# Strips' maxima combined by one reduction, softmax sums in two levels, and a new order table, in a fused attention and mixture-of-experts kernel

## The chip, the core and the metric

The kernel runs on one core of one Trainium2 chip. The metric is the device time of one execution in microseconds. TensorE is called PE below, VectorE DVE, ScalarE ACT, GpSimd POOL and SyncE SP, as in the profile. PSUM is the memory that PE writes, in eight banks; SBUF is the main on-chip memory.

## What is computed

Two attentions with 32 inducing points, and then a mixture of experts on the result. B = 4 batches of N = 11456 tokens, C = 128 channels, m = 32, E = 8 experts, F = 1024.

```python
def _attn_ref(x, inducing):
    def mab(q, kv):
        s = scale * (q @ kv.transpose(0, 2, 1))
        s = s - s.max(-1, keepdims=True)
        a = np.exp(s)
        a /= a.sum(-1, keepdims=True) + 1e-09
        return a @ kv
    h = mab(I, x)          # first attention: 32 queries over all tokens
    return mab(x, h)       # second attention: every token over 32 keys

def _moe_ref(x, w_skip, w_gate, w1, w2):   # x: the attention's output, all tokens
    do_compute = x @ w_skip > 0
    # a token that computes takes its best expert e of x @ w_gate:
    # out = x + prob_e * relu(x @ w1[e]) @ w2[e]; the others: out = x
```

## The kernel before

**Tiling.** A batch is cut into six groups of 2048 tokens (the last has 1216). The tokens of a group are laid out as four strips of 32 rows each, so that the 32 inducing points of every strip fill the 128 partitions. Most steps take two groups at once (1024 columns in each partition).

**First attention** (`first`), 13 steps in all: four in batch 0, whose first two groups go singly, and three in each other batch. A step is: scores on PE (L397, L400), the largest score of each partition on DVE (`maxima`, L404, stored negated in a column of the small tile `mins`), the combination of the four strips' values and of the older minimum into one value for each of the 32 rows and its spread back to all 128 partitions (`least`, L409 to L418, six short DVE instructions: copies of 64 and 32 rows to other partitions and element-wise minima), the exponentials on ACT with that value as bias (L421, and L424 for the factor that rescales older sums), a transpose of 32x32 blocks on DVE (L431), transposes of x on PE (L439) copied out by ACT or DVE (`copy`, L344 and L346), sums on PE (L453), and their addition to `acc` on DVE (L462).

**Middle** (`middle`), once for each batch: h from `acc` (PE L502, DVE L506, L507), the expert that the batch mostly takes, its weights by two DMAs on SP's queue (`load_w`, L665, L667), and the expert's image of the 32 rows of h.

**Second attention** (`second`), 13 steps: scores (L692), transpose to tokens on DVE (L696), greatest of each token's 32 (L700), its subtraction (`less`, L708, in two halves, one for each group, on POOL or DVE), exponentials on ACT into the tile `texp` (L711), the sums of 32 values and a constant 1e-9 as a 33rd column on DVE (`total`, L715), the reciprocal (L717), the scaling (`norm`, L721, two halves on POOL or DVE), a transpose (L726), the gate logits and gate (L734 to L776), a second scaling (`scale2`, L782, two halves) and transpose (L726), and `emit`: the output's sums on PE (L822), the copies out of PSUM, and the stores on SP's queue.

**Order.** Nothing is scheduled by the compiler. `ORDER` holds, for each engine, the numbers of the steps in the order in which that engine's instructions stand; which engine runs a step with a choice (`less`, `norm`, `scale2`, copies out of PSUM) follows from the list in which its number stands. `placed` replays these lists with the costs that each step is given, and so chooses the PSUM banks and buffers. The costs (`both`, `dve`, `act` and the dictionaries at `L.add`) choose nothing else: the engines run their lists in order on the chip and wait for each other by semaphores. `awake` puts idle matmuls ahead of a PE step where that replay shows a gap on PE.

Of the kernel before, what the change touches and what calls it, by code (L numbers as in the profile page):

```python
# [1168 lines left out]
```

## Time and profile before

| | before |
|---|---|
| median of 3 runs | 200.16 us (199.42 to 200.36) |
| the profiled execution | 199.29 us, span 197.3 us |
| busy, of the span | PE 178.8 us (91%), DVE 166.3 (84%), ACT 119.5 (61%), POOL 102.1 (52%) |
| granted TensorE clock | 0.99 of full speed, mean |
| DMA | 51.54 MB, mean 261 GB/s |

The span runs from the first to the last instruction of the profiled execution; 2.0 us of its time lie outside the span. The page gives busy times, the chain that ended last, and groups of instructions by line; the trace behind it gives each stretch of time, each line and each wait. Matmuls overlap, so PE's busy time holds some time in which PE drains.

### The profile page before, as it was taken

The page shows a single profiled execution, that of the slowest core. Times are in us where ns is not written, and L with a number is a line of the kernel's source. Part 1 is how long each engine was busy: PE and PEld are TensorE (multiplying, and loading weights), DVE is VectorE, ACT ScalarE, POOL GpSimd, SP SyncE. Part 2 cuts the span into 40 slices and gives each one's busy share as a digit, 9 for nine tenths or more (in the row PEclk, how much of TensorE's full clock was granted, in tenths as well). Part 3 has the DMA queues.
Part 4 walks back from the last instruction along what each step waited for, and adds up shares of the span by engine and source line. Part 5 has one row for each costly group of instructions (what it writes and reads, how often), then busy time and mean ns, then how long its engine had stood idle before and what let it go on. Part 6 is the DMA issues. An engine that isn't in the chain of part 4 may idle for free. (4 is left out here: it accounts for less than half of the span.)

```text
span 197.3 us, 5919 instructions
## 1 busy us (share of the span) xinstructions
PE 178.8 (91%) x2353; PEld 111.3 (56%) x2354; DVE 166.3 (84%) x367; ACT 119.5 (61%) x179; POOL 102.1 (52%) x194
## 2 busy tenths in 40 slices
PE   7997999997999899999889998999999959999972
PEld 7565667445874755756466356677435334453641
DVE  0699788899999999999999979998988983998641
ACT  3215324334876583884759539765959557789780
POOL 8000000274449561988456177656987895567430
PEclk9999999999999999999999999999999996999999
DMA  6999990199900003999903949375189998798996
GB/s 211 374 420 403 410 379 23 40 397 388 404 16 5 3 0 118 327 399 394 389 21 112 381 154 325 130 196 223 71 350 357 279 401 343 308 355 324 406 375 233
DMA packets 16317, 51.54 MB, mean 261 GB/s; under 512 B 1952, under 2 KB 4000, under 8 KB 16288
## 3 DMA queue, kind: packets, MB, share of 16 engines
q1 hardware_dynamic: 16000, 51.12, 69.1%
q8 instruction: 19, 0.31, 0.6%
q14 instruction: 10, 0.08, 0.1%
q10 hardware_dynamic: 288, 0.02, 0.1%
HBM read 27.68 MB, written 23.46 MB: 259 GB/s over the span
## 5 line engine op out<-in xcount | busy, mean ns | idle before, releaser
L344 ACT COPY o<-bank 128x1024 f32<-128x1024 f32 (+1 forms) x48 | 44.3, 961 | 15.6 <-PE bank L822 8.7
L439 PE MATMUL bank<-ident,x 128*128 128x128 f32 x360 | 47.3, 279 | 2.2 <-DVE e L696 1.4
L344 ACT COPY xt<-bank 128x1024 f32<-128x1024 f32 (+3 forms) x44 | 37.3, 889 | 13.0 <-PE bank L439 7.0
L439 PEld LDWEIGHTS bank<-ident,x 128*128 128x128 f32 x360 | 39.4, 141 | 9.9 <-issue 2.8
L822 PE MATMUL bank<-x,hr 32*128 32x512 f32 (+1 forms) x192 | 27.8, 615 | 3.6 <-ACT o L344 2.8
L708 POOL TENSOR_TENSOR e<-e,ts 128x512 f32<-128x512 f32 (+1 forms) x24 | 23.9, 1011 | 13.4 <-DVE ts L700 12.0
L721 POOL TENSOR_TENSOR e<-texp,ts 128x512 f32<-128x512 f32 (+1 forms) x24 | 23.9, 1012 | 11.3 <-DVE ts L717 10.2
L726 DVE STREAM_TRANSPOSE x<-e 128x1024 f32<-128x1024 f32 (+3 forms) x26 | 28.4, 1098 | 1.5 <-POOL e L782 0.9
L421 ACT ACTIVATE a<-bank,mins 128x1024 f32<-128x1024 f32 (+3 forms) x13 | 13.0, 1003 | 23.7 <-DVE mins L418 23.7
L453 PE MATMUL bank<-xt,a1T 128*32 128x129 f32 x720 | 24.9, 274 | 1.6 <-DVE a1T L431 1.4
L822 PE MATMUL bank<-x,yr 32*128 32x512 f32 (+1 forms) x192 | 26.2, 580 | 0.1
L453 PEld LDWEIGHTS bank<-xt,a1T 128*32 128x32 f32 x720 | 20.0, 110 | 9.7 <-issue 5.6
L782 POOL TENSOR_TENSOR e<-e,gs 128x512 f32<-128x512 f32 (+1 forms) x20 | 20.4, 1032 | 7.1 <-DVE gs L346 4.0
L397 PE MATMUL bank<-x,iT_sb 128*32 128x512 f32 (+1 forms) x192 | 22.0, 567 | 1.5 <-DMA x<-in_xT_dram 0.7
L692 PE MATMUL bank<-x,hc 128*32 128x512 f32 (+1 forms) x192 | 22.3, 578 | 0.1
L587 POOL TENSOR_SCALAR r<-codes,code,lr 128x7 f32<-128x7 f32 x4 | 1.7, 425 | 33.0 <-DVE lr L577 33.0
L696 DVE STREAM_TRANSPOSE e<-bank 128x1024 f32<-128x1024 f32 (+3 forms) x13 | 14.4, 1111 | 4.7 <-ACT o L344 3.0
L822 PEld LDWEIGHTS bank<-x,hr 32*128 32x128 f32 x192 | 9.7, 188 | 13.3 <-ACT o L344 4.6
L711 ACT ACTIVATE texp<-e 128x1024 f32<-128x1024 f32 (+3 forms) x13 | 12.6, 968 | 7.0 <-DVE e L696 4.3
L822 PEld LDWEIGHTS bank<-x,yr 32*128 32x128 f32 x192 | 11.0, 191 | 9.7 <-issue 8.5
L431 DVE STREAM_TRANSPOSE a1T<-a 128x1024 f32<-128x1024 f32 (+3 forms) x13 | 14.2, 1094 | 1.4 <-ACT a L421 1.3
L404 DVE TENSOR_REDUCE mins<-bank 128x1 f32<-128x1024 f32 (+3 forms) x13 | 13.7, 1057 | 1.4 <-PE bank L397 1.2
(132 smaller groups left out, 229.8 us busy)
## 6 DMA issues: line engine op xcount, KB each, us to landing
x<-in_xT_dram SPq DMA_DIRECT2D x40, 512.0 KB, 9.1
out_dram<-o SPq DMA_DIRECT2D x40, 512.0 KB, 3.6
out_dram<-o SPq DMA_DIRECT2D x8, 304.0 KB, 5.0
w1s<-in_w_dram SPq DMA_DIRECT2D x4, 512.0 KB, 5.0
w2s<-in_w_dram SPq DMA_DIRECT2D x4, 512.0 KB, 5.2
x<-in_xT_dram SPq DMA_DIRECT2D x4, 320.0 KB, 5.1
x<-in_xT_dram SPq DMA_DIRECT2D x4, 288.0 KB, 4.4
iT_sb<-in_iT_dram ACTq DMA_DIRECT2D x1, 16.0 KB, 3.0
```

Of the source, the lines that this page charges most:

```text
L344: nc.scalar.copy(out=out, in_=in_)
L397: nc.tensor.matmul(ps[q * M:(q + 1) * M, off[i]:off[i] + G.kf * M], lhsT=iT_sb, rhs=x[:, q], start=True, stop=True)
L431: nc.vector.transpose(out=st["aT"][:, 0:W], in_=st["a"][:, 0:W])
L439: nc.tensor.transpose(out=at(buf)[0:w, j * P:(j + 1) * P], in_=s.x[gs[i]][:, k * P:k * P + w], identity=ident)
L453: nc.tensor.matmul(ph[k % Q * M:(k % Q + 1) * M, 0:P + 1], lhsT=st["aT"][:, c:c + M], rhs=flat(i)[:, k, :], start=(i == 0 and k < Q), stop ...
L692: nc.tensor.matmul(ps[q * M:(q + 1) * M, off[i]:off[i] + G.w2], lhsT=s.hc[:, 0:M], rhs=s.x[g][:, G.s2[q]:G.s2[q] + G.w2], start=True, stop ...
L696: nc.vector.transpose(out=st["e"], in_=st["ps"][:, 0:W])
L708: on(o).tensor_tensor(out=v, in0=v, in1=part(st["mx"], i), op=ALU.subtract)
L721: on(o).tensor_tensor(out=blocks(st["e"], i), in0=texps[bex.idx][:, t0:t0 + Gs[i].nb, 0:M], in1=part(st["i"], i), op=ALU.mult)
L726: nc.vector.transpose(out=u[:, 0:W], in_=st["e"])
L782: on(o).tensor_tensor(out=v, in0=v, in1=gm.unsqueeze(3).broadcast_to([P, Q, v1 - v0, M]), op=ALU.mult)
L822: nc.tensor.matmul(at(bp[q // 2])[:, p0:p0 + G.w1], lhsT=m[r, :], rhs=st[k][r, c], start=(k == "u1"), stop=(k == "u2"))
```

## The change

**The combination of maxima.** `mins` gets Q + 2 = 6 columns and is made one step ahead. `maxima` still writes column 0. A new step `gather` copies the values of strips 1 to 3 into columns 1 to 3 of the first 32 partitions (three copies of 32x1, on POOL or ACT). `least` is one DVE reduction over these columns and, except in a batch's first step, over column 4, where the step before left its minimum. A new step `spread` copies the result to the other three strips, and, except after a batch's last step, into column 4 of the next step's tile (three or four copies of 32x1, on POOL or ACT).

**The sums of the second attention.** `texp` holds each token's 32 exponentials as two halves of 16, with a 17th column each (1e-9 and 0). A new POOL step `fold` adds the two halves, 17 columns for each token, into `e`, and `total` reduces 17 columns instead of 33.

**Weights.** The two weight DMAs become two steps of SP's list; the first product waits for the first alone in the planner.

**Order and costs.** `ORDER` is new in every engine's list, and some costs are changed.

```diff
     "DVE": """
-9 14 4 5 16 7 21 26 28 13 22 45 24 38 39 30 48 41 60 61 63 65 72 70 52 203 74 204 76 77 79 80 206 82 85 97 98 128
+4 11 6 16 30 9 23 25 32 15 28 51 42 44 54 18 47 34 66 68 71 58 78 215 82 217 84 85 87 220 106 107 88 108 239 138 139
...
-    texps = [const.tile([P, PB, M + 1], F32, name=f"texp{i}") for i in range(BUFS["ex"])]
+    texps = [const.tile([P, PB, 2, M // 2 + 1], F32, name=f"texp{i}") for i in range(BUFS["ex"])]
     for t in texps:
-        nc.gpsimd.memset(t[:, :, M:M + 1], 1e-9)
+        nc.gpsimd.memset(t[:, :, 0, M // 2:], 1e-9)
+        nc.gpsimd.memset(t[:, :, 1, M // 2:], 0.0)
...
+        def gather(o):
+            for q in range(1, Q):
+                copy(o, mins[0:M, q:q + 1], mins[q * M:(q + 1) * M, 0:1])
+
         def least(o):
-
-            m, v = mins[:, 0:1], mins[:, 2:4]
-            nc.vector.tensor_copy(out=v[0:2 * M, 0:1], in_=m[2 * M:4 * M])
-            nc.vector.tensor_tensor(out=v[0:2 * M, 1:2], in0=m[0:2 * M], in1=v[0:2 * M, 0:1], op=ALU.min)
-            nc.vector.tensor_copy(out=v[0:M, 0:1], in_=v[M:2 * M, 1:2])
-            if one:
-                nc.vector.tensor_tensor(out=bias[0:M], in0=v[0:M, 0:1], in1=v[0:M, 1:2], op=ALU.min)
-            else:
-                nc.vector.tensor_scalar(out=bias[0:M], in0=v[0:M, 0:1], scalar1=v[0:M, 1:2], scalar2=old[0:M],
-                                        op0=ALU.min, op1=ALU.min)
-            nc.vector.tensor_copy(out=bias[M:2 * M], in_=bias[0:M])
-            nc.vector.tensor_copy(out=bias[2 * M:4 * M], in_=bias[0:2 * M])
+            nc.vector.tensor_reduce(out=bias[0:M], in_=mins[0:M, 0:Q if one else Q + 1], axis=AX.X, op=ALU.min)
+
+        def spread(o):
+            for q in range(1, Q):
+                copy(o, bias[q * M:(q + 1) * M], bias[0:M])
+            if gs[-1] < NG - 1:
+                copy(o, after[0:M, Q:Q + 1], bias[0:M])
...
-        s.lastm = o = L.add({"DVE": 0.86}, least, o, s.lastm)
+        o = L.add({"POOL": 0.45, "ACT": 0.6}, gather, o)
+        s.lastm = o = L.add({"DVE": 0.2}, least, o, s.lastm)
+        s.lastm = o = L.add({"POOL": 0.5, "ACT": 0.75}, spread, o)
...
-        o_w = L.add({"SP": 1.6}, weights, o, take=[bw], size=1048.0)
+        o_w = [L.add({"SP": c}, lambda o, k=k: weights(o, k), o, take=[bw] if k == 1 else [], size=524.0)
+               for k, c in ((1, 0.6), (2, 0.95))]
...
         def exps(o):
-            nc.scalar.activation(out=ev(M), in_=blocks(st["e"]), func=AF.Exp, scale=scale)
+            nc.scalar.activation(out=ev(), in_=halved(blocks(st["e"])), func=AF.Exp, scale=scale)
+
+        def fold(o):
+            v = texps[bex.idx][:, 0:nb]
+            st["half"] = st["e"][:, 0:nb * (M // 2 + 1)].rearrange("p (t m) -> p t m", m=M // 2 + 1)
+            nc.gpsimd.tensor_tensor(out=st["half"], in0=v[:, :, 0, :], in1=v[:, :, 1, :], op=ALU.add)
 
         def total(o):
             r = sums[:, b, base]
-            nc.vector.tensor_reduce(out=r, in_=ev(M + 1), axis=AX.X, op=ALU.add)
+            nc.vector.tensor_reduce(out=r, in_=st["half"], axis=AX.X, op=ALU.add)
```

**Where instructions move.** The rows below are instructions as they stand in the built program: line, operation, output and inputs with the program's names, partitions x elements, and in brackets the engines that are waited for. Line numbers of after are its own. `mins_0_180` and `mins_0_166` are the `mins` tiles of batch 1's first step; `e`, `ts`, `texp` and `sums` are tiles of the second attention.

DVE at the end of batch 0's first attention, where `acc` is completed and the middle begins; before:

```order
L404 TENSOR_REDUCE mins_0_180<-bank_67 128x1 [waits PE_49]
L462 SCALAR_TENSOR_TENSOR acc_287<-acc_287,f_0_4_420,bank_69 128x129 [waits DVE_49,PE_49]
L409 COPY mins_0_180<-mins_0_180 64x1 [waits DVE_49]
L410 TENSOR_TENSOR mins_0_180<-mins_0_180 64x1 [waits DVE_49]
L411 COPY mins_0_180<-mins_0_180 32x1 [waits DVE_49]
L413 TENSOR_TENSOR mins_0_180<-mins_0_180 32x1 [waits DVE_49]
L417 COPY mins_0_180<-mins_0_180 32x1 [waits DVE_49]
L418 COPY mins_0_180<-mins_0_180 64x1 [waits DVE_49]
L506 TENSOR_SCALAR den_525<-bank_69 128x1 [waits PE_49]
```

The same place after:

```order
L409 TENSOR_REDUCE mins_0_166<-bank_68 128x1 [waits PE_49]
L466 SCALAR_TENSOR_TENSOR acc_297<-acc_297,f_0_4_435,bank_70 128x129 [waits DVE_49,PE_49,Activation_49]
L416 TENSOR_REDUCE mins_0_166<-mins_0_166 32x1 [waits DVE_49,Activation_49]
L512 TENSOR_SCALAR den_537<-bank_70 128x1 [waits PE_49]
L513 RECIPROCAL den_537<-den_537 128x1 [waits DVE_49]
```

Six DVE instructions between the last addition to `acc` and the denominator have become one, which waits for ACT's three copies.

POOL in batch 2's first step, between the gate scalings of batch 0 (L797), after; DVE's list has L409 and L416 of `mins_0_170` one behind the other there:

```order
L797 TENSOR_TENSOR e_0_1_561<-e_0_1_561,gs_0_139 128x384 [waits Activation_49]
L352 COPY mins_0_170<-mins_0_170 32x1 [waits DVE_49,Pool_49]
L352 COPY mins_0_170<-mins_0_170 32x1 x2
L352 COPY mins_0_170<-mins_0_170 32x1 [waits DVE_49]
L352 COPY mins_0_170<-mins_0_170 32x1 x2
L352 COPY mins_2_189<-mins_0_170 32x1
L797 TENSOR_TENSOR e_0_1_561<-e_0_1_561,gs_0_139 128x512 [waits Pool_49]
```

Gather and spread of that step now stand in POOL's list, between the two halves of one scaling.

DVE in the second attention of batch 1's first pair, after (before, both halves of `less` of this pair stood on POOL):

```order
L705 STREAM_TRANSPOSE e_1_0_1044<-bank_70 128x1024 [waits PE_49,Activation_49]
L709 TENSOR_REDUCE ts_0_131<-e_1_0_1044 128x32 [waits DVE_49]
L717 TENSOR_TENSOR e_1_0_1044<-e_1_0_1044,ts_0_131 128x512 [waits DVE_49]
L705 STREAM_TRANSPOSE e_1_2_1084<-bank_67 128x1024 [waits PE_49,Activation_49]
L741 STREAM_TRANSPOSE x_148<-e_0_4_640 128x1024 [waits DMAHW5_49,Pool_49]
L709 TENSOR_REDUCE ts_1_133<-e_1_2_1084 128x32 [waits DVE_49]
L464 COPY acc_1156<-bank_69 128x129 [waits PE_49,Activation_49]
L729 TENSOR_REDUCE sums<-e_1_0_1044 128x32 [waits Pool_49]
```

POOL at the same place after:

```order
L717 TENSOR_TENSOR e_1_0_1044<-e_1_0_1044,ts_0_131 128x512 [waits DVE_49]
L725 TENSOR_TENSOR e_1_0_1044<-texp_126 128x544 [waits Activation_49]
L717 TENSOR_TENSOR e_1_2_1084<-e_1_2_1084,ts_1_133 128x512 [waits DVE_49]
L736 TENSOR_TENSOR e_1_0_1044<-texp_126,ts_0_132 128x512 [waits DVE_49,Pool_49]
```

One half of `less` has moved from POOL to DVE, the fold (L725) has come in on POOL, and DVE's sum (L729) now waits for POOL instead of ACT. Over the whole program DVE's wide element-wise instructions (`less`, `norm`, `scale2`) go from 4 to 14 and POOL's from 68 to 58; 53 of the 87 short copies stand on POOL and 34 on ACT; DVE's full copies of transposed x go from 7 to 5 and ACT's from 33 to 35.

## Rows read from the trace of the kernel before

**Rows 1.** Page, part 1: busy time, share of the span, instructions of each engine.

```profile
PE 178.8 (91%) x2353; PEld 111.3 (56%) x2354; DVE 166.3 (84%) x367; ACT 119.5 (61%) x179; POOL 102.1 (52%) x194
```

**Rows 2.** Stretches between denominators (L507): length, busy per engine, clock, DMA, GB/s.

```profile
0.00:33.10 33.10, 30.09 (x376) 22.24 (x377) 23.76 (x58) 9.92 (x17) 4.16 (x37) 1.00 0.85 331
33.10:68.20 35.10, 31.57 (x472) 21.17 (x471) 32.47 (x70) 20.62 (x31) 17.37 (x28) 1.00 0.46 176
68.20:104.30 36.10, 34.04 (x499) 22.27 (x497) 34.73 (x71) 24.72 (x39) 24.16 (x39) 1.00 0.61 226
104.30:139.00 34.70, 33.53 (x499) 21.47 (x501) 32.12 (x68) 23.90 (x35) 19.86 (x31) 1.00 0.63 216
139.00:197.30 58.30, 49.62 (x521) 24.14 (x513) 43.22 (x104) 40.34 (x61) 36.55 (x63) 0.97 0.85 322
```

**Rows 3.** Groups by form, the combination: xcount | busy us, mean ns | idle before.

```profile
L409 DVE COPY mins<-mins 64x1 f32<-64x1 f32 x13 | 1.9, 149 | 0.4
L410 DVE TENSOR_TENSOR mins<-mins 64x1 f32<-64x1 f32 x13 | 3.7, 288 | 0.4
L413 DVE TENSOR_TENSOR mins<-mins 32x1 f32<-32x1 f32 x4 | 1.9, 472 | 0.1
L415 DVE TENSOR_SCALAR mins<-mins,mins 32x1 f32<-32x1 f32 x9 | 2.3, 259 | 0.3
L417 DVE COPY mins<-mins 32x1 f32<-32x1 f32 x13 | 1.9, 143 | 0.5
```

**Rows 4.** Groups by form: the shortest instructions like the added ones.

```profile
L573 DVE TENSOR_REDUCE lm<-own 128x1 f32<-128x8 f32 x4 | 0.6, 162 | 0.1
L859 DVE TENSOR_REDUCE lom<-bank 1x1 f32<-1x128 f32 x4 | 1.0, 273 | 0.4 <-PE bank L855 0.4
L590 POOL COPY r<-lr 128x1 f32<-128x1 f32 x4 | 0.7, 184 | 0.0
L424 ACT ACTIVATE f<-mins,mins 128x1 f32<-128x1 f32 x9 | 2.6, 288 | 0.0
```

**Rows 5.** Groups by form: reductions on DVE, two-input instructions on POOL.

```profile
L715 DVE TENSOR_REDUCE sums<-texp 128x32 f32<-128x1056 f32 x8 | 9.9, 1232 | 0.0
L715 DVE TENSOR_REDUCE sums<-texp 128x16 f32<-128x528 f32 x1 | 0.7, 694 | 0.0
L708 POOL TENSOR_TENSOR e<-e,ts 128x512 f32<-128x512 f32 x20 | 20.7, 1047 | 10.7 <-DVE ts L700 10.7
L766 POOL TENSOR_TENSOR lt<-lt,gs 128x128 f32<-128x128 f32 x8 | 4.2, 527 | 5.9 <-DVE lo L852 4.2 <-DVE gs L763 1.6
```

**Rows 6.** Groups by form: work that the order moves, at its price on DVE.

```profile
L782 DVE TENSOR_TENSOR e<-e,gs 128x512 f32<-128x512 f32 x4 | 2.8, 696 | 0.1
L346 DVE COPY xt<-bank 128x1024 f32<-128x1024 f32 x7 | 8.3, 1216 | 0.5 <-PE bank L439 0.5
```

**Rows 7.** Timeline, DVE and POOL side by side: start us, us, instruction, idle before.

```profile
99.69 1.05 POOL L782 TENSOR_TENSOR e<-e,gs 128x512 f32<-128x512 f32 x1 [0.28 <-ACT gs L344]
100.03 0.72 DVE L410 TENSOR_TENSOR mins<-mins 64x1 f32<-64x1 f32 x1
...
170.73 0.69 DVE L782 TENSOR_TENSOR e<-e,gs 128x512 f32<-128x512 f32 x1
170.78 1.55 POOL L782 TENSOR_TENSOR e<-e,gs 128x512 f32<-128x512 f32 x1 [0.38 <-DVE gs L346]
```

**Rows 8.** Timeline of the first stretch: PE's longest wait, and its end.

```profile
16.16 1.09 PE L453 MATMUL bank<-xt,a1T 128*32 128x129 f32 x32 [1.18 <-DVE a1T L431]
...
31.43 0.34 DVE L462 SCALAR_TENSOR_TENSOR acc<-acc,f,bank 128x129 f32<-128x129 f32 x1
31.96 0.39 PE L502 MATMUL bank<-acc,rep 128*128 128x129 f32 x2
32.88 0.16 DVE L506 TENSOR_SCALAR den<-bank 128x1 f32<-128x1 f32 x1
```

**Rows 9.** Timeline in the last stretch, PE alone: the output's sums.

```profile
161.29 1.14 PE L822 MATMUL bank<-x,hr 32*128 32x512 f32 x8 [1.86 <-ACT o L344]
163.51 1.95 PE L822 MATMUL bank<-x,hr 32*128 32x512 f32 x8
```

More of the change, by code (lines that the diff above doesn't have):

```diff
@@ L304 @@
         s.groups = split(b)
+        s.mins = const.tile([P, Q + 2], F32, name=f"mins_{b}_0")
         twos = [(g, g + 1) for g in range(0, NG - 1, 2)] + ([(NG - 1,)] if NG % 2 else [])
@@ L329, in both @@
     def both(w):
-        return {"POOL": 0.2 + 0.0018 * w, "DVE": 0.22 + 0.0011 * w}
+        return {"POOL": 0.16 + 0.00175 * w, "DVE": 0.22 + 0.0011 * w}
     def act(w):
@@ L382, in first @@
         off = [sum(G.k1 * M for G in Gs[:i]) for i in range(n)]
-        old = None if one else s.mins[:, 1:2]
-        mins = s.mins = const.tile([P, 4], F32, name=f"mins_{b}_{gs[0]}")
-        bias = mins[:, 1:2]
+        old = None if one else s.mins[:, Q + 1:Q + 2]
+        mins = s.mins if one else s.after
+        s.mins, s.after = mins, const.tile([P, Q + 2], F32, name=f"mins_{b}_{gs[-1] + 1}")
+        after, bias = s.after, mins[:, Q + 1:Q + 2]
         bs, bh = Buf(kind), Buf("ps")
@@ L558, in expert, with weights @@
             st["e"] = nc.values_load(st["ei"][0:1, 0:1], engines=(SP,), min_val=0, max_val=E - 1)
-        def weights(o):
-            st["w1"], st["w2"] = load_w(st["e"], f"{b}")
+        def weights(o, k):
+            st[f"w{k}"] = load_w(k, st["e"], f"{b}")
         bw = Buf("w")
         o = L.add({"SP": 1.05}, expert, o_c)
-        o_w = L.add({"SP": 1.6}, weights, o, take=[bw], size=1048.0)
+        o_w = [L.add({"SP": c}, lambda o, k=k: weights(o, k), o, take=[bw] if k == 1 else [], size=524.0)
+               for k, c in ((1, 0.6), (2, 0.95))]
         def relative(o):
@@ L600, in g_of @@
                                  rhs=st["w1"][:, j * (F // Q):(j + 1) * (F // Q)], start=True, stop=True)
[L602 removed]
+        o, f = mm(0.43, TILE, g_of, "gr", s.o_hc, o_w[0])
         def g_rows(o):
@@ L644, in y_of @@
                                  start=(k < Q), stop=(k >= KF - Q))
-        o, f = mm(0.43, TILE, y_of, "yp", o_g, o_w)
+        o, f = mm(0.43, TILE, y_of, "yp", o_g, o_w[1])
         o.free = [bw, bg]
@@ L661, in middle, with load_w @@
         return L
-    def load_w(e, name):
-        w1s = wk.tile([P, F], F32, tag="w1s", bufs=1, name=f"w1s_{name}")
-        nc.sync.dma_start(out=w1s, in_=w1[bass.ds(e, 1), :, :].rearrange("o c f -> c (o f)"))
-        w2s = wk.tile([P, F], F32, tag="w2s", bufs=1, name=f"w2s_{name}")
-        nc.sync.dma_start(out=w2s, in_=w2[bass.ds(e, 1)].rearrange("o p k c -> p (o k c)"))
-        return w1s, w2s
+    def load_w(k, e, name):
+        w = wk.tile([P, F], F32, tag=f"w{k}s", bufs=1, name=f"w{k}s_{name}")
+        if k == 1:
+            nc.sync.dma_start(out=w, in_=w1[bass.ds(e, 1), :, :].rearrange("o c f -> c (o f)"))
+        else:
+            nc.sync.dma_start(out=w, in_=w2[bass.ds(e, 1)].rearrange("o p k c -> p (o k c)"))
+        return w
     def second(s, gs):
@@ L684, in second @@
         blocks = lambda v, i=None: (v if i is None else v[:, off[i]:off[i] + Gs[i].w2]).rearrange("p (t m) -> p t m", m=M)
-        ev = lambda n: texps[bex.idx][:, 0:nb, 0:n]
+        ev = lambda: texps[bex.idx][:, 0:nb, :, 0:M // 2]
+        halved = lambda v: v.rearrange("p t (h m) -> p t h m", h=2)
         def scores(o):
@@ L720, in norm @@
             t0 = off[i] // M
-            on(o).tensor_tensor(out=blocks(st["e"], i), in0=texps[bex.idx][:, t0:t0 + Gs[i].nb, 0:M], in1=part(st["i"], i),
+            v = part(st["i"], i).rearrange("p t (h m) -> p t h m", h=2)
+            on(o).tensor_tensor(out=halved(blocks(st["e"], i)), in0=texps[bex.idx][:, t0:t0 + Gs[i].nb, :, 0:M // 2], in1=v,
                                 op=ALU.mult)
@@ L789, in second @@
         o = L.add({"ACT": 0.22 + 0.00085 * W}, exps, *os, take=[bex])
-        o = L.add({"DVE": dve(W * 33 / 32)["DVE"] + 0.19 + 0.006 * nb}, total, o)
+        o = L.add({"POOL": 0.2 + 0.0018 * W * 17 / 32}, fold, o)
+        o = L.add({"DVE": dve(W * 17 / 32)["DVE"] + 0.19 + 0.006 * nb}, total, o)
         s.o_total.append(o)
@@ L802, in second @@
         o = L.add({"ACT": 0.19, "DVE": 0.19}, gates_in, o, free=[bm])
-        os = [L.add({"POOL": 0.2 + 0.00185 * G.w2, "DVE": 0.2 + 0.0011 * G.w2}, lambda o, i=i: scale2(o, i), o) for i, G in enumerate(Gs)]
+        os = [L.add({"POOL": 0.17 + 0.00178 * G.w2, "DVE": 0.2 + 0.0011 * G.w2}, lambda o, i=i: scale2(o, i), o) for i, G in enumerate(Gs)]
         o_2 = L.add(dve(W), lambda o: back(2), *os, free=[be, blt])
@@ L954, in other @@
         nc.vector.tensor_copy(out=main, in_=own("code"))
-        w1s, w2s = load_w(e, "o")
+        w1s, w2s = (load_w(k, e, "o") for k in (1, 2))
         nc.vector.tensor_copy(out=code, in_=codes[:, bass.ds(e, 1)])
@@ L979, in other_part @@
         blocks = e.rearrange("p (t m) -> p t m", m=M)
-        ev = texps[0][0:M, 0:nb, :]
+        ev = texps[0][0:M, 0:nb].rearrange("p t h m -> p t (h m)")
+        main = texps[0][0:M, 0:nb, :, 0:M // 2]
+        halved = lambda v: v.rearrange("p t (h m) -> p t h m", h=2)
         mx, inv = low(MAXB), low(MAXB)
@@ L990, in other_part @@
         nc.vector.tensor_tensor(out=blocks, in0=blocks, in1=wide(mx), op=ALU.subtract)
-        nc.scalar.activation(out=ev[:, :, 0:M], in_=blocks, func=AF.Exp, scale=scale)
+        nc.scalar.activation(out=main, in_=halved(blocks), func=AF.Exp, scale=scale)
         nc.vector.tensor_reduce(out=inv[:, 0:nb], in_=ev, axis=AX.X, op=ALU.add)
         nc.vector.reciprocal(out=inv[:, 0:nb], in_=inv[:, 0:nb])
-        nc.vector.tensor_tensor(out=blocks, in0=ev[:, :, 0:M], in1=wide(inv), op=ALU.mult)
+        nc.vector.tensor_tensor(out=halved(blocks), in0=main, in1=halved(wide(inv)), op=ALU.mult)
         nc.vector.transpose(out=u1, in_=e)
```

1 line of the change is left out of this document (removed), and 58 rows, old and new, of the table ORDER.

## The prediction

> **What bounds the kernel now.** I read the page's busy times first, then the stretches between the four denominators, then the groups of the lines that change, then the timeline where two engines meet. The page gives PE 178.8 us and DVE 166.3 us of a 197.3 us span, with ACT and POOL far behind [rows 1]. An average hides where each one binds, so I cut the span at the denominators (L507), where a batch passes from the first attention to the second [rows 2]. I call the stretches A to E. A (33.10 us) is batch 0's first attention: PE is busy 30.09 us, DVE 23.76. In B, C and D (35.10, 36.10 and 34.70 us) the second attention of one batch runs beside the first attention of the next: DVE is busy 32.47, 34.73 and 32.12 us, PE 31.57, 34.04 and 33.53. In C DVE is 96% busy, in D PE is 97% busy. In E (58.30 us) only second attentions are left: PE 49.62, DVE 43.22, ACT 40.34. So DVE and PE bind together in B to D; a shorter DVE list helps there only by PE's idle time, which is 3.53, 2.06 and 1.17 us. In E DVE does not bind.
>
> **The change part by part.** *Combination of maxima.* Removed from DVE, in each of 13 steps: copies of about 0.145 us four times (L409 and L417 shown, L411 and L418 like them), L410 at 0.288, and L413 at 0.472 (4 steps) or L415 at 0.259 (9 steps) [rows 3]: 13 x (0.58 + 0.288) + 4 x 0.472 + 9 x 0.259 = 15.5 us. Added on DVE: 13 reductions of 32 x 4 or 5 values, between 0.162 (128 x 8) and 0.273 us (1 x 128 from PSUM) [rows 4]; I take 0.165, since the first is nearest in size: 2.1 us (at most 3.5). Net -13.4 us. Added elsewhere: 53 copies on POOL, nearest row 0.184 us, 9.8 us; 34 on ACT, between DVE's 0.145 for the same move [rows 3] and ACT's 0.288 for one column [rows 4], 5 to 10 us. A copy that crosses partitions on POOL has no row; below 0.184 nothing on POOL speaks for it, and twice that would be 19.5 us.
>
> *The wait that this adds.* Before, DVE ran the whole combination alone, in 1.1 us where nothing blocked it (31.77 to 32.88 [rows 8]). Now DVE's reduction waits for three copies of another engine: a hand-over takes at most the 0.19 us from the end of the last addition at 31.77 to PE's product at 31.96 [rows 8], I take 0.1 for each, and 0.18 for each copy: 0.7 us, and once more for the spread. Maximum to exponentials takes about 1.6 us, 0.5 more. On DVE all that stands behind L416 waits. In the order four of the 13 have it directly behind its maximum, three of them in A, one in C: 4 x 0.7 = 2.8 us of DVE. The others have between one short copy and eight instructions in between. On POOL and ACT the copies stand among wide instructions of about 1.05 us, so a copy can be held that long, and DVE with it.
>
> *Sums in two levels.* A reduction costs 1.232 us for 1056 columns and 0.694 for 528 [rows 5], so 0.71 for 544 by the same slope: -0.52 x 8, -0.46 x 3 for the pairs of 924 columns, and about -0.46 for the last two, in all -6.0 us of DVE. POOL gets 13 folds. The nearest row is a two-input instruction of 512 columns, 1.047 us; with the rate of the short-run one, 0.527 us for 128 columns [rows 5], a fold of 544 could take 1.7. I take 1.15, because its runs of 17 are nearer to the first's 32 than to the second's 8: 8 x 1.15 and 4.4 for the five smaller, 13.6 us (12.5 to 19). The fold lengthens the chain exponentials, sum, scaling by 0.6 us; three `e` buffers hide it in B to D, nothing does at the kernel's end, where the last group's is some 0.5 us.
>
> *The order table.* DVE gets ten more wide halves at 0.696 (one and a fraction of them smaller), 6.9 us, and loses two copies of transposed x at 1.216, -2.4 [rows 6]; small moves (three gate copies, one output copy of 608 columns, one four-instruction chain, one scaling of h) add about 2.3. In sum DVE changes by -13.4 - 6.0 + 6.9 - 2.4 + 2.3 = -12.6 us, to about 154. POOL: 102.1 + 9.8 + 13.6 - 10.5 (ten halves) - 1 = 114, 58% of the span. ACT: 119.5 + 7.5 + 2 (two copies of x) - 1.5 = 127.5. PE's work is the same in every stretch, as are its counts. The weights' DMAs carry the same bytes and stand in the same region of SP's list, where the first product needs only the first of them: I cost that at nothing, since the products have most of a stretch of other work around them.
>
> *What of it is on the path, by stretch.* A: DVE loses about 4.0 (combinations) and 2.4 (copies), and waits 2.1 more at L416. PE's list sets the stretch; of its 3.0 us idle 1.1 lie before its first matmul, and its longest wait, 1.18 us, is for a DVE transpose [rows 8]. At the end six instructions stand between the last addition, done at 31.77, and the denominator at 32.88, while PE's product (from 31.96, 0.39 us) could have released it at about 32.4 [rows 8]. At most 1.9 + 0.5; I take 1.5. B: three combinations (-3.4) and three sums (-1.5) against three halves (+2.1), PE idle 3.53: I take 1.5. C: three combinations, two of them blocked ones (-4.0), two sums (-1.0), against one half, gate copies and one gate that comes earlier (+1.8) and the wait of 0.7; PE idle 2.06: I take 1.5. D: two combinations (-1.9), three sums (-1.5) against three halves and the moved chain (+3.1): 0.3. E: DVE and POOL stay about equal and the same work is left; what can go is PE's wait of 1.86 us before 161.29, after which eight matmuls took 1.95 us instead of 1.14 [rows 9] in a stretch with a mean granted clock of 0.97 of the full 2.4 GHz, where it is 1.00 before [rows 2]: 0.3. Sum 1.5 + 1.5 + 1.5 + 0.3 + 0.3 = 5.1 us. From the profiled 199.29 that is 194.2; the median of before lies 0.87 above that execution, so **195.1 us**.
>
> **The rivals.** *The shared access.* At 99.69 POOL began a wide instruction of 1.05 us; DVE's L410 with 64 x 1 values began at 100.03 and took 0.72, until POOL's ended, where its other executions take 0.15. At 170.73 it was the other way: DVE's wide one ran its 0.69, and POOL's, begun 0.05 later, took 1.55 instead of about 1.05 [rows 7]. The Trainium skill says why, in "SBUF — State Buffer", section "Who interferes with whom": a DVE instruction with two SBUF inputs and a POOL instruction that reads SBUF share one port pair as an exclusive lock, and the later one blocks; and "Perfetto Trace Analysis", section "Optimizing Scalar/DVE Operations", adds that moving work between the two might therefore not help. The rows agree; by that rule the sum comes out at this rival's time, by the mean of the wide ones at the forecast's. The change takes 17 small such DVE instructions away, which lost 13 x 0.138 + 4 x 0.32 = 3.1 us to it [rows 3], and puts ten wide ones in, beside a POOL that is busier. Against a large loss: the four wide ones of before took 0.696 in the mean. If the 14 lose 0.35 each (a third of a wide POOL instruction) and POOL 0.5, most of the gain of B to D goes: 1 us of it is left, 1 in A, none in E: 199.29 + 0.87 - 1.9 = 198.3.
>
> *PE binds all along.* D shows 97%. Then only A's end moves: 199.7.
>
> *Slower: DVE stands at L416.* The eight combinations in B to D lie among wide POOL and ACT instructions. DVE's net relief there is -3.4 - 4.0 - 1.9 - 4.0 + 7.0 = -6.3 us plus 0.7 of known wait; the mechanism decides from 0.7 us of mean extra wait at each of the eight. With a full wide instruction ahead of each (1.05 + 0.7) DVE is 8 us worse, of which I pass on the same half as above, less A's 1 us: 199.29 + 0.87 + 3 - 1 = 202.2. For it: in batch 2's first step the gather stands on POOL behind a scaling that itself waits for ACT's gate copy. Against it: most have one to three long DVE instructions in between, and three of the four that have none stand in A, where POOL is idle.
>
> *More than that.* If PE's idle time in B to D goes altogether (6.8 us), with A's 1.9 and 0.8 in E: 199.29 + 0.87 - 9.5 = 190.7.
>
> **How the numbers follow.** Forecast (192.5 to 197.5): 0.47. More (below 192.5): 0.12. Shared access (197.5 to 199.2): 0.15. PE binds (within 0.5%, 199.2 to 201.2): 0.11. Slower: 0.15. A half per cent, 1.0 us, is about what a measurement can tell here, as the three runs differ by 0.94. Faster is 0.47 + 0.12 + 0.15 = 0.74, same 0.11, slower 0.15. The range goes from 190.0, under the full PE case (0.05 lies below), to 201.0 (0.15 above). The doubled prices of POOL's copies and folds (10 and 5 us of POOL, which would then be 65% busy) lie inside it, because they act through the waits of the shared-access and the slower rival.
>
> **What would show it.** DVE about 154 us busy; the reductions L416 near 0.17 us, L729 near 0.71, folds near 1.15; the denominators at about 31.6, 65.2, 99.8 and 134.2 us; the last stretch about 58. Shared access shows as wide DVE halves well above 0.70 and POOL ones above 1.05. The slower rival shows as DVE's idle time in front of L416, put down to POOL or ACT copies, of more than 5 us. If the copies of 32 x 1 on POOL cost well over 0.2 us, or if B to D do not shrink although DVE's list is shorter, the prediction is wrong.

## The result and the profile after

The changed kernel takes 194.27 us (median of 194.21, 194.27 and 194.61) against 200.11 us of the kernel before, which ran beside it: a ratio of 0.972, 95% interval 0.9685 to 0.9751. In a second timing it took 196.31 us (four executions, 196.09 to 196.78) against 199.5 us: 0.982, interval 0.977 to 0.987. The forecast was 195.1 us. Disturbed executions are left out of all times and ratios (two of five in the first timing, 198.69 and 251.27 us, and one each of e3, its profiled one, and e12 below), and as the profiled one of the first timing was among them, all rows of the changed kernel are from the second, from an execution of 196.45 us. There is no trace of an execution of 194 us, and what makes those 2 us of difference stays open. Timings are compared below by their ratio to the kernel before, which ran beside each. As one and the same kernel gives 0.972 and 0.982, a difference of 1 point (2 us) between two timings shows nothing by itself.

Part 1 of the page of the changed kernel (busy time, share of the span, instructions), beside [rows 1]:

```profile
PE 176.8 (91%) x2360; PEld 111.2 (57%) x2361; DVE 155.1 (80%) x319; ACT 126.6 (65%) x210; POOL 118.1 (61%) x248
```

DVE has 11.2 us less (12.6 forecast), ACT 7.1 more (8.0), POOL 16.0 more (12). Cut at the four denominators (now L513), as [rows 2] (length, busy time and instructions of each engine, clock, DMA share, GB/s):

```profile
0.00:32.90 32.90, 29.37 (x372) 21.58 (x374) 17.53 (x31) 14.14 (x35) 6.74 (x53) 1.00 0.92 358
32.90:63.27 30.37, 29.80 (x453) 20.71 (x451) 27.08 (x56) 20.94 (x35) 19.30 (x40) 1.00 0.50 186
63.27:98.94 35.67, 35.11 (x510) 22.55 (x509) 32.19 (x60) 26.61 (x46) 27.57 (x49) 1.00 0.61 219
98.94:135.56 36.62, 33.67 (x510) 22.53 (x512) 33.67 (x67) 24.28 (x39) 26.14 (x46) 1.00 0.59 206
135.56:194.50 58.94, 48.85 (x528) 23.82 (x520) 44.59 (x107) 40.59 (x59) 38.36 (x63) 0.97 0.83 318
```

| stretch | forecast | measured | PE idle before, after |
|---|---|---|---|
| A | -1.5 | -0.2 | 3.0, 3.5 |
| B | -1.5 | -4.7 | 3.5, 0.6 |
| C | -1.5 | -0.4 | 2.1, 0.6 |
| D | -0.3 | +1.9 | 1.2, 2.9 |
| E | -0.3 | +0.6 | 8.7, 10.1 |

The five sum to -2.8 us between these two executions. About 1.3 us of B's gain is moved work: 19 of its 472 matmuls, at 31.57 / 472 us each, now stand later. By the fourth denominator PE has done the same number (1845 against 1846) and is 3.4 us ahead; E gives 0.6 back.

The groups of the changed lines, by form (xcount | busy us, mean ns | idle before), beside [rows 3 to 6]:

```profile
L352 POOL COPY mins<-mins 32x1 f32<-32x1 f32 x53 | 9.7, 183 | 33.6 <-DVE mins L416 16.5 <-DVE mins L409 14.4 <-DVE lm L580 1.0
L348 ACT COPY mins<-mins 32x1 f32<-32x1 f32 x34 | 6.4, 190 | 11.6 <-DVE mins L409 7.3 <-DVE mins L416 3.9
L416 DVE TENSOR_REDUCE mins<-mins 32x1 f32<-32x5 f32 x9 | 1.2, 132 | 2.1 <-ACT mins L348 1.4 <-POOL mins L352 0.7
L416 DVE TENSOR_REDUCE mins<-mins 32x1 f32<-32x4 f32 x4 | 0.6, 145 | 1.2 <-POOL mins L352 0.8 <-ACT mins L348 0.4
L729 DVE TENSOR_REDUCE sums<-e 128x32 f32<-128x544 f32 x8 | 5.6, 704 | 0.4 <-POOL e L725 0.4
L725 POOL TENSOR_TENSOR e<-texp 128x544 f32<-128x544 f32 x8 | 9.6, 1198 | 6.9 <-ACT texp L720 6.8
L717 DVE TENSOR_TENSOR e<-e,ts 128x512 f32<-128x512 f32 x7 | 5.9, 840 | 0.1
L797 DVE TENSOR_TENSOR e<-e,gs 128x512 f32<-128x512 f32 x5 | 3.7, 739 | 0.1
L736 DVE TENSOR_TENSOR e<-texp,ts 128x512 f32<-128x512 f32 x1 | 1.1, 1110 | 0.0
```

The prices of the sum hold: copies 0.183 us on POOL and 0.190 on ACT, the reductions 0.132 to 0.145 and 0.704, a fold 1.2. DVE is idle 3.3 us before L416 (2.1 + 1.2), of which 2.8 was forecast, and 0.4 before the eight wide sums. Only the wide halves are dearer: DVE's than their 0.696, and POOL's by about 3 us in all, most of the 4 us by which POOL's busy time exceeds the forecast.

### The profile page after: what moved, and what is told of

It is laid out like the page before. It is cut to its first block, busy times and chain, and to the rows that moved or that the text cites. A ratio compares the mean times of both kernels' runs of the same rounds, so it can differ in the third digit from the quotient of the medians.

```text
span 196.8 us, 5985 instructions
## 1 busy us (share of the span) xinstructions
PE 177.2 (90%) x2360; PEld 111.2 (57%) x2361; DVE 154.9 (79%) x319; ACT 126.5 (64%) x210; POOL 118.3 (60%) x248
## 4 chain that ended last, share of the span: by engine, by line
PE 45%; DMA 20%; DVE 11%; ACT 9%; POOL 6%; issue 5%; SPq 1%; ACTq 0%; DVEq 0%; POOLq 0%
DMA x<-in_xT_dram 12%; PE bank L443 11%; DMA out_dram<-o 8%; PE bank L701 8%; PE bank L838 8%; PE bank L402 7%; PE bank L457 5%; ACT o L348 5%; ACT xt L348 2%; DVE e L705 2%; POOL e L797 2%; DVE x L741 1%; POOL e L725 1%; DVE mins L409 1%; DVE ts L709 1%
## 5 line engine op out<-in xcount | busy, mean ns | idle before, releaser
L348 ACT COPY o<-bank 128x1024 f32<-128x1024 f32 (+1 forms) x47 | 43.5, 964 | 14.0 <-PE bank L838 9.3
L443 PE MATMUL bank<-ident,x 128*128 128x128 f32 x360 | 48.2, 279 | 2.0 <-ACT xt L348 0.8
L348 ACT COPY xt<-bank 128x1024 f32<-128x1024 f32 (+3 forms) x46 | 39.4, 890 | 7.5 <-PE bank L443 7.3
L352 POOL COPY mins<-mins 32x1 f32<-32x1 f32 x53 | 9.8, 184 | 34.3 <-DVE mins L416 16.6
L838 PE MATMUL bank<-x,hr 32*128 32x512 f32 (+1 forms) x192 | 26.8, 612 | 1.2 <-ACT yr L348 0.5
L838 PE MATMUL bank<-x,yr 32*128 32x512 f32 (+1 forms) x192 | 25.0, 578 | 0.0
L717 POOL TENSOR_TENSOR e<-e,ts 128x512 f32<-128x512 f32 (+1 forms) x17 | 17.8, 1054 | 11.8 <-DVE ts L709 6.3
L736 POOL TENSOR_TENSOR e<-texp,ts 128x512 f32<-128x512 f32 (+1 forms) x22 | 23.1, 1063 | 1.3 <-DVE ts L731 1.2
L797 POOL TENSOR_TENSOR e<-e,gs 128x512 f32<-128x512 f32 (+1 forms) x19 | 20.4, 1082 | 5.7 <-DVE gs L350 3.9
L409 DVE TENSOR_REDUCE mins<-bank 128x1 f32<-128x1024 f32 (+3 forms) x13 | 13.9, 1067 | 9.6 <-PE bank L405 4.9
L725 POOL TENSOR_TENSOR e<-texp 128x544 f32<-128x544 f32 (+3 forms) x13 | 14.4, 1106 | 7.9 <-ACT texp L720 7.8
L720 ACT ACTIVATE texp<-e 128x1024 f32<-128x1024 f32 (+3 forms) x13 | 12.6, 967 | 9.9 <-POOL e L717 8.4
L838 PEld LDWEIGHTS bank<-x,yr 32*128 32x128 f32 x192 | 10.8, 191 | 9.4 <-issue 8.7
```

The lines of the kernel that those rows point to most:

```text
L348: nc.scalar.copy(out=out, in_=in_)
L443: nc.tensor.transpose(out=at(buf)[0:w, j * P:(j + 1) * P], in_=s.x[gs[i]][:, k * P:k * P + w], identity=ident)
L717: on(o).tensor_tensor(out=v, in0=v, in1=part(st["mx"], i), op=ALU.subtract)
L725: nc.gpsimd.tensor_tensor(out=st["half"], in0=v[:, :, 0, :], in1=v[:, :, 1, :], op=ALU.add)
L736: on(o).tensor_tensor(out=halved(blocks(st["e"], i)), in0=texps[bex.idx][:, t0:t0 + Gs[i].nb, :, 0:M // 2], in1=v, op=ALU.mult)
L797: on(o).tensor_tensor(out=v, in0=v, in1=gm.unsqueeze(3).broadcast_to([P, Q, v1 - v0, M]), op=ALU.mult)
```

## The experiments

"The way" is the time from the end of a maximum (L409) to the start of the exponentials that wait for its combination, worked out from the timelines and summed over the 13 combinations. "Stand" is DVE's idle time before the short reduction. In the table the changed kernel (its second timing), e2, e3 and e4 were timed on one chip, e5 to e8 on another, e9 to e12 on a third.

| kernel | ratio to before (95%) | DVE, POOL busy, us | way | stand |
|---|---|---|---|---|
| before | 1 | 166.3, 102.1 | 29.2 | none |
| changed | 0.982 (0.977 to 0.987) | 155.1, 118.1 | 33.2 | 3.3 |
| e2_old_comb | 1.027 (1.019 to 1.035) | 167.9, 108.3 | 35.1 | none |
| e3_old_sums | 0.984 (0.979 to 0.990) | 160.4, 104.1 | 33.2 | 3.3 |
| e4_order_only | 1.035 (1.030 to 1.041) | 173.2, 94.1 | 35.8 | none |
| e5_comb_old_order | 0.983 (0.978 to 0.988) | 153.5, 117.6 | 30.5 | 8.4 |
| e6_both_old_order | 1.028 (1.024 to 1.033) | 148.0, 130.7 | 30.9 | 8.2 |
| e7_halves_pool | 0.980 (0.974 to 0.986) | 150.1, 122.3 | 33.4 | 3.3 |
| e8_copies_twice | 1.034 (1.028 to 1.040) | 155.0, 126.3 | 48.8 | 9.3 |
| e10_spread_twice | 1.003 (0.999 to 1.006) | 155.0, 123.0 | 42.7 | 3.3 |
| e9_two_copies | 0.970 (0.965 to 0.975) | 155.6, 115.4 | 29.5 | 2.3 |
| e11_two_copies_halves | 0.973 (0.968 to 0.977) | 149.3, 119.6 | 30.2 | 2.3 |
| e12_two_copies_old_order | 0.972 (0.967 to 0.977) | 153.7, 113.3 | 26.8 | 6.8 |

**The parts in the new order.** The changed kernel again, and three kernels that differ from it in the arithmetic alone.

> The changed kernel again, unedited, for a profiled execution at the speed of its usual times. By the usual times so far (194.2 to 194.6 us) its span is 192.3 to 192.6 us. My sum by stretch puts the denominators at 31.6, 65.2, 99.8 and 134.2 us and the last stretch at 58; if the gain sits elsewhere than I said, these are the numbers that miss.

```diff
 # e2: the combination of before, in the place of the one reduction (gather and spread are empty)
-            nc.vector.tensor_reduce(out=bias[0:M], in_=mins[0:M, 0:Q if one else Q + 1], axis=AX.X, op=ALU.min)
+            m, v = mins[:, 0:1], mins[:, 2:4]
+            nc.vector.tensor_copy(out=v[0:2 * M, 0:1], in_=m[2 * M:4 * M])
...
 # e3: no fold, 33 columns reduced
-            nc.gpsimd.tensor_tensor(out=st["half"], in0=v[:, :, 0, :], in1=v[:, :, 1, :], op=ALU.add)
+            st["half"] = v.rearrange("p t h m -> p t (h m)")[:, :, 0:M + 1]
 # e4: both
```

> The changed kernel's order and sums, but the strips' maxima combined as before, by six DVE instructions in the place of the one (the copies on POOL and ACT are gone). My theory, that DVE's relief by the combinations is what pays: DVE busy up by about 13 us, time up by 3 to 4.5 us, to about 198. Rival, that the rest of the order table pays and the wait at the short reduction eats the combination's gain: at most 1 us above the changed kernel, about 195 or below it. Denominator of batch 0: by my theory 1.5 us later than in the changed kernel.

> The changed kernel's order and combination, but the second attention's sums in one level: no fold on POOL, DVE reduces 33 columns a block (1056 a pair) as before. My theory: DVE up by 6 us, POOL down by 13 to 14, the chain from exponentials to scaling shorter by 0.6 us where nothing hides it; time up by 1 to 2 us, about 195.8. Rival, that the folds cost through POOL (which holds DVE's two-input instructions and the halves behind them) what they save: no change or a gain, 194.3 or below.

> The changed kernel's order of work, with both the combination and the sums as before: what the order table does alone. My theory: DVE has the ten more halves and all of its old work, busy about 172 us; 199.5 to 202, as the kernel before or slower. Rival, that the order itself (PE's list, the weights' two steps) pays: 196 or below. If the two parts add up, the distance from the changed kernel is the sum of the two single ones.

With the old combination the kernel takes 205.5 us, 4.5% of 199.5 or 9.0 us above the changed kernel, where 3 to 4.5 were expected. DVE is 12.8 us busier and the way hardly longer (35.1 against 33.2), but exponentials wait longer for DVE behind them: from their end to the start of the transpose the thirteen sum to 36.3 us against 29.3. So in this order DVE's added time comes out at 0.7 us a us. With the old sums the ratio is 0.984, 0.4 us more, where 1 to 2 were expected; the intervals 0.979 to 0.990 and 0.977 to 0.987 overlap, so what the sums give here is not settled, and it may be nothing. The order alone is 7.0 us slower than the kernel before by the ratio (medians 207.29 and 199.5; 199.5 to 202 was expected): without the new arithmetic it loses. It is 10.6 us above the changed kernel; the two parts taken singly make 9.4.

**The parts in the old order.** Next the other way round: the new arithmetic in the order table of before.

```diff
 # e5: before's ORDER and one-level sums; one step issues all of the combination, the copies on POOL
+            for q in range(1, Q):
+                nc.gpsimd.tensor_copy(out=mins[0:M, q:q + 1], in_=mins[q * M:(q + 1) * M, 0:1])
+            nc.vector.tensor_reduce(out=bias[0:M], in_=mins[0:M, 0:Q if one else Q + 1], axis=AX.X, op=ALU.min)
+            for q in range(1, Q):
+                nc.gpsimd.tensor_copy(out=bias[q * M:(q + 1) * M], in_=bias[0:M])
...
 # e6: and the two-level sums, the fold on POOL directly ahead of the sum
```

> The kernel before with its own order table and one-level sums, and only the combination changed: where DVE ran six instructions, POOL now copies three columns, DVE reduces, POOL copies back, in the same place of every list. So POOL's copies stand where its list happened to be. My theory (DVE's relief pays, the copies' wait is small): DVE busy down by 13 us, time down by 2 to 5 us against the kernel before. Rival (the slower case of my prediction): the copies are held behind POOL's wide instructions, DVE idles more than 5 us before the short reduction, and the time is the same or longer than before.

> The same with the two-level sums as well, still in the order table of before; the fold stands on POOL where the sum stood on DVE. My theory: DVE busy down by 19 us; 1 us less than the run with the combination alone, as in the new order (where the sums gave about 1 us). Rival: the folds land behind POOL's wide halves and DVE waits for them, so it is slower than the run with the combination alone. The distance from the changed kernel is what the new order table is worth once the arithmetic is new; with the order alone at 7.8 us slower than before, I expect 1 to 4 us.

The combination alone, without a new order or a fold, gives 0.983: all that the whole change gives in the second timing. (The tile `texp` has the changed kernel's layout in e5, e6 and e12; that changes no price: the wide sums take 1.227 us against 1.232, the exponentials 1.064 against 1.069.) It does so although DVE stands 8.4 us before its reduction, more than the 5 us at which I had expected the slower rival to win; it is still 12.8 us less busy, so 4.4 us are left. With the folds added the same table is 9 us slower, at DVE's lowest busy time of all, 148.0 us. The waits of that kernel say why (who waited for whom: us in total, times, longest):

```profile
DVE sums L733 <- POOL e L729: 19.6, 13, 3.6
```

Before each sum DVE stands for a fold that is itself behind POOL's wide halves, 1.5 us on average, against 1.1 us in all in the changed kernel. What the new order table brings is this: a place for the fold. With both parts of the arithmetic new it is worth 4.6 points, 9 us, where 1 to 4 were expected. Table and fold together bring nothing measurable beyond what the combination gives alone (0.982 and 0.983, from two chips; e9 and e12 below ask the same on one chip).

**What a change of DVE's busy time is worth.**

```diff
 # e7: steps 108, 140, 172, 306, 534, 535, 566 (less) leave DVE's list and stand beside their partners on POOL's
-69 218 109 111 141 242 ... 266 173 146 ... 305 308 ... 636 386 507 508 ... 515 567 519
+69 218 108 109 111 140 141 242 ... 266 172 173 146 ... 305 306 308 ... 636 386 534 535 507 508 ... 515 566 567 519
```

> The changed kernel, but the seven halves of the subtraction of maxima that its table gives to DVE go back to POOL, next to their partners. DVE busy down by about 5.9 us (seven at 0.84), POOL up by about 7.3. If DVE's busy time still sets the pace (my sum passes on half): 2 to 3 us faster, about 194. If shared access eats the exchange (the lock rival): faster too, and POOL's wide ones fall towards 1.05 us each. If what counts is that two halves run side by side, since the exponentials wait for both: slower, by up to 7 x 0.5 us, about 198 to 199.

DVE has 5.0 us less, POOL 4.2 more, and the ratio is 0.980 against 0.982: no difference that these timings can show, and e11 beside e9, on one chip, shows none either (0.973 and 0.970). POOL rises by less than the 7.3 us of the seven halves, because its other wide halves of `less` fall from 1.087 us to 1.048. So in the changed kernel shortening DVE's list at POOL's cost gives nothing. The exponentials' waits point to one reason (e7's row, then the changed kernel's):

```profile
ACT texp L716 <- POOL e L713: 11.4, 7, 4.3
```

```profile
ACT texp L720 <- POOL e L717: 8.3, 5, 3.7
```

Two halves in a row on POOL end later than two side by side. How much of DVE's relief that ate is not separated by this run.

**What the way is worth.** Both copies doubled, the spread's alone doubled, and fewer copies.

```diff
 # e8 (gather and spread), e10 (spread alone): every copy issued twice
-            for q in range(1, Q):
+            for q in (1, 2, 3, 1, 2, 3):
 # e9: gather by 64 x 1 and 32 x 2, spread by 32 x 1 and 64 x 1
+            copy(o, mins[0:2 * M, 1:2], mins[2 * M:4 * M, 0:1])
+            copy(o, mins[0:M, 2:4], mins[M:2 * M, 0:2])
...
+            copy(o, bias[M:2 * M], bias[0:M])
+            copy(o, bias[2 * M:4 * M], bias[0:2 * M])
 # e11: e9 and e7; e12: the same copies in e5, all on POOL
```

> The changed kernel with each of the copies of a combination issued twice (three extra in the gather, three in the spread), which lengthens the way from maximum to exponentials by about 1.1 us thirteen times and DVE's wait before the short reduction by about 0.55 where nothing lies in between. My theory (eight of the thirteen have other work in between): DVE's idle time before the short reduction grows from 3.3 to about 6 us, time up by 1 to 2 us. Rival (the wait decides from 0.7 us a place): 4 us or more, back at the kernel before.

> The changed kernel with only the spread's three copies issued twice, which come after DVE's reduction and hold DVE at no place; the gather stays. The way from maximum to exponentials grows by about 0.55 us thirteen times, 7.2 us. If the length of that way is what counts, about half of the 10.3 us of both doublings: 5 us more than the changed kernel. If what counted there was DVE standing at the short reduction (its idle time grew by 6.0 us), 1 to 2 us more.

> The changed kernel with two copies for the gather (64 x 1, then 32 x 2) and two for the spread (32 x 1, then 64 x 1) in place of three and three: 26 copies of 0.18 us fewer, each of the 13 ways from maximum to exponentials shorter by about 0.36 us. The run with the copies twice lengthened the 13 ways by 15.6 us in sum and took 10.3 us more, 0.66 for each. Theory now (the way from maximum to exponentials is on the path): 13 x 0.36 x 0.66 = 3.1 us faster than the changed kernel, 193. Rival (the path does not get shorter any more, as it did not with the halves back on POOL): within 1 us of it. A dependent copy may cost more than an independent one; then less than 3.

> Both: two copies each way, and the seven halves of the subtraction back on POOL. The halves alone changed nothing (0.980 of the kernel before against 0.982). Theory: the same 3 us as the two copies alone, 192.5 to 193. Rival, that POOL's list, then over 120 us, holds the copies: slower than with two copies alone by 1 us or more.

> The order table and the one-level sums of before, only the combination changed, now with two copies each way on POOL (64 x 1 and 32 x 2; 32 x 1 and 64 x 1) round DVE's one reduction. With three copies each way this was 0.983 of the kernel before. Theory (the way from maximum to exponentials is on the path at 0.66 us a us): 13 x 0.36 us less of it, about 3 us, 0.968, as fast as or faster than the changed kernel without any new order or fold. Rival (after the first gain PE's list and the arrival of x bind, which no shorter DVE list moved): 0.980 to 0.985 again; the new order would then be what lets two copies pay.

One combination of batch 0 in four kernels, from the timelines of DVE, ACT and POOL (start us, us, instruction, idle before). The kernel before does it on DVE alone:

```profile
21.07 1.23 DVE L404 TENSOR_REDUCE mins<-bank 128x1 f32<-128x1024 f32 x1
...
23.34 0.15 DVE L418 COPY mins<-mins 64x1 f32<-64x1 f32 x1
23.61 1.12 ACT L421 ACTIVATE a<-bank,mins 128x1024 f32<-128x1024 f32 x1 [2.98 <-DVE mins L418]
```

The changed kernel:

```profile
21.67 1.23 DVE L409 TENSOR_REDUCE mins<-bank 128x1 f32<-128x1024 f32 x1 [1.23 <-PE bank L402]
22.93 0.59 ACT L348 COPY mins<-mins 32x1 f32<-32x1 f32 x3 [2.92 <-DVE mins L409]
23.61 0.15 DVE L416 TENSOR_REDUCE mins<-mins 32x1 f32<-32x5 f32 x1 [0.71 <-ACT mins L348]
23.82 0.61 POOL L352 COPY mins<-mins 32x1 f32<-32x1 f32 x3 [5.81 <-DVE mins L416]
24.46 1.12 ACT L425 ACTIVATE a<-bank,mins 128x1024 f32<-128x1024 f32 x1 [0.94 <-POOL mins L352]
```

With the copies twice (e8), and with two copies each way (e9):

```profile
25.76 1.26 ACT L348 COPY mins<-mins 32x1 f32<-32x1 f32 x6 [1.59 <-DVE mins L409]
27.11 0.15 DVE L416 TENSOR_REDUCE mins<-mins 32x1 f32<-32x5 f32 x1 [1.38 <-ACT mins L348]
```

```profile
22.92 0.41 ACT L348 COPY mins<-mins 64x1 f32<-64x1 f32 x2 [2.47 <-DVE mins L409]
23.42 0.15 DVE L416 TENSOR_REDUCE mins<-mins 32x1 f32<-32x5 f32 x1 [0.54 <-ACT mins L348]
23.63 0.41 POOL L352 COPY mins<-mins 32x1 f32<-32x1 f32 x2 [5.18 <-DVE mins L416]
24.07 1.11 ACT L425 ACTIVATE a<-bank,mins 128x1024 f32<-128x1024 f32 x1 [0.74 <-POOL mins L352]
```

The maximum ends at 22.30 before, at 22.90 after and at 22.89 with two copies, so the way is 1.31 us, 1.56 us and 1.18 us. Each hand-over costs little (0.03 to 0.09 us from one engine's end to the other's start); the six copies are what makes it longer than before.

My theory, that most combinations have other work in between and the copies' time is hidden, fell with e8, for which 1 to 2 us more were expected. Twice the copies take 5.2 points of the ratio, 10.3 us, for 15.6 us of way. e10 splits it: the spread alone lengthens the way by 9.5 us, DVE's stand at the reduction not at all, and costs 2.0 points, 4.1 us, 0.4 for each us of way. What the doubled gather adds to that is 6.1 us of way, all but 0.1 of it stand (9.3 against 3.3), and 6.2 us of time: about one us of the kernel for each us that DVE stands. These differences cross chips. Within one chip, e10 lies 3.3 points (6.6 us) above e9 for 13.2 us more way, 0.9 of it stand, and e8 5.4 points (10.8 us) above e7 for 15.4 us, 6.0 of it stand. Solved together, these two pairs give 0.46 for a us of the other way and 1.1 for a us of stand, so within a chip the rates come out alike. They are estimates: the doubled copies also keep POOL and ACT busier (8.2 and 4.8 us in e8), which no run separates. In e10 DVE stands one step later instead, before it transposes the exponentials, 5.8 us in all instead of 3.2 in the changed kernel. Most of that is in the wide transposes (the changed kernel's row, then e10's):

```profile
L435 DVE STREAM_TRANSPOSE a1T<-a 128x1024 f32<-128x1024 f32 x8 | 9.8, 1231 | 2.8 <-ACT a L425 2.8
```

```profile
L435 DVE STREAM_TRANSPOSE a1T<-a 128x1024 f32<-128x1024 f32 x8 | 9.8, 1231 | 4.8 <-ACT a L425 4.8
```

Whether shortening pays too is not shown. Two copies for three give 1.2 points in the new order (0.982 to 0.970) and 1.1 in the old one (0.983 to 0.972), each for 3.7 us less way: 2.5 and 2.2 us, where 3 were expected. But both kernels with two copies ran on one chip, both with three on others, and the changed kernel itself differs by 1.0 point between its two timings; against the first (0.9685 to 0.9751) e9 is not faster. What one chip does show is e12 beside e9: the kernel before with nothing changed but the combination is as fast (0.972, interval 0.967 to 0.977) as the kernel that has the fold and the new table besides (0.970, 0.965 to 0.975).

## Why the prediction was right, and where it was not

**The total and the direction** held: 195.1 forecast, 194.3 and 196.3 measured. **The reason** held in its main term: the combinations give the gain, in the new order (e2) and in the old one (e5). DVE's sum was -11.2 us, not -12.6, and most of the difference is the wide halves. **The split by stretch** did not hold, and that the total came out owes something to luck: no stretch but E is within 1 us of its forecast, and B's 3.2 us too much pay for more than half of the 5.5 us that A, C, D and E miss. In the traced execution the five sum to -2.8 us against the -5.1 of the forecast; the first timing came out at -5.8.

**A, -1.5 forecast, -0.2 measured: the step "PE's list sets the stretch" failed.** PE's wait for a DVE transpose at 16.16 [rows 8] is gone, and PE gets to the same product at 14.78. It then stands for x itself. PE's timeline of the changed kernel:

```profile
14.78 1.06 PE L457 MATMUL bank<-xt,a1T 128*32 128x129 f32 x32
15.77 1.97 PE L443 MATMUL bank<-ident,x 128*128 128x128 f32 x16
19.68 1.92 PE L402 MATMUL bank<-x,iT_sb 128*32 128x512 f32 x16 [1.95 <-DMA x<-in_xT_dram]
```

The DMA share of 0.85 in A, in [rows 2], was the hint that I left out; now it is 0.92. I had asked which wait goes, not which is late next. The end of A came as forecast. From the end of the last addition to the denominator it took 1.11 us and takes 0.61 now (32.09 to 32.70). DVE stands 0.40 us before L416 there, but that costs next to nothing, since the denominator's product on PE ends only at 32.67:

```profile
32.28 0.39 PE L508 MATMUL bank<-acc,rep 128*128 128x129 f32 x2
32.49 0.14 DVE L416 TENSOR_REDUCE mins<-mins 32x1 f32<-32x4 f32 x1 [0.40 <-ACT mins L348]
32.70 0.16 DVE L512 TENSOR_SCALAR den<-bank 128x1 f32<-128x1 f32 x1
```

What misses is all before it: the last addition, which ended at 31.77, ends at 32.09 now, although DVE has 6.2 us less to do in A.

**B, -1.5 forecast, -4.7 measured: mis-sized.** Nearly all of PE's idle time went (3.5 to 0.6 us) where I let less than half of it go, and 1.3 us of PE's work moved on to later stretches, where I had called its work the same in every stretch. DVE's work moved as well: it is 5.4 us less in B, where my terms sum to 2.8. **C** followed: PE's idle time fell by 1.5 us as forecast, with 11 matmuls more in it.

**D, -0.3 forecast, +1.9 measured: what the order moved there outweighs what the two combinations and three sums take away.** DVE's busy time in D rose from 32.12 to 33.67 us, PE has 11 matmuls more, and it stands for 1.0 us (for ACT) and 1.1 us (for DVE), where its longest waits for these two were 0.66 and 0.23 before. PE's timeline:

```profile
123.45 1.09 PE L457 MATMUL bank<-xt,a1T 128*32 128x129 f32 x32 [1.02 <-ACT xt L348]
...
131.85 1.09 PE L457 MATMUL bank<-xt,a1T 128*32 128x129 f32 x32 [1.12 <-DVE a1T L435]
```

**E, -0.3 forecast, +0.6 measured: the wait changed its name.** Instead of standing 1.86 us for ACT's output copy [rows 9], PE stands for ACT's copy of `g`, and the clock falls behind it as it did:

```profile
157.28 0.48 PE L619 MATMUL bank<-ident,g 128*128 128x128 f32 x2 [1.19 <-ACT g L348]
157.69 2.09 PE L838 MATMUL bank<-x,hr 32*128 32x512 f32 x8
```

The granted clock is 0.57 of the full 2.4 GHz from 157 to 161 us, mostly its lower level of 1.2 GHz, and the eight matmuls take 2.09 us where they took 1.95 before.

**The wait at L416** was sized rightly in the kernel that was built (3.3 us against 2.8) and wrongly in its rate. I passed on half of DVE's waits; e8 and e10 give about one for one, and 0.4 for the spread, which I had sized at 0.5 us a time and charged nowhere. (That rival's sum is off by 1 us too: half of its 8 us is 4, which makes 203.2 and not 202.2.) So the slower rival was nearer than its 15% suggest: 0.46 us of extra stand at each of 13 places, with the longer spread, puts the kernel 3.4% behind the one before. What kept it away: in the kernel as built only five of the 13 reductions stand at all, for at most 0.8 us.

**The sums** save DVE 6.2 us (14.4 to 8.2) as forecast (6.0), but e3 shows 0.4 us of the time for them, which is not clear of nothing, and e12, which has no fold, is as fast as e9. The sentence that three `e` buffers hide the fold holds only with the new table; in the old one DVE stands 19.6 us for it.

**The shared access** is there and is small: 14 wide halves on DVE take 11.3 us; at 0.69 (and 0.56 for the one of 384 columns) they would take 9.5, so 1.8 us against the 4.9 of that rival. POOL's 58 wide halves take about 3 us more than at their means of before. With the seven halves back on POOL (e7) about two thirds of both losses are gone, and the time is the same within the noise. **PE binds all along** did not come: C is at 98% now, but B, C and D together are shorter by 3.2 us.

## What to carry to other kernels

When a serial step is taken off a busy engine and given to another, count the way that its consumers wait as well as the engine's time: here an engine that stands for a neighbour's copy cost about as much as if it worked, and a longer way behind it cost about half as much. Time each part alone in the old order before a new order is drawn up: one part carried all of the gain that could be measured. A folded reduction needs a place on the helping engine's list before it is due; put in the old place, 6 us of saving came with 19.6 us of standing. Before a wait is credited as gain, look for what is late next at that place, transfers among it.
